# A SwiGLU layer on one core: the two x loads of the head on one queue, the Silu table load ahead of a weight load, and two filler matmuls removed

## The chip, the core and the metric

The kernel runs on one core of a Trainium2 chip. The core has a matrix engine (TensorE, PE in the profile, whose weight loads have a row of their own, PEld), VectorE (DVE), ScalarE (ACT), GpSimd (POOL), SyncE (SP) and 16 DMA engines. A transfer is issued by an instruction on SP, ACT or POOL; each of the three has its own DMA queue (q1, q10 and q0 in the profile), and the same 16 engines serve all three.

The metric is the device time of one execution in microseconds. Before the change it is 163.57 us (median of 3 runs, 163.47 to 163.64).

## The reference

The inputs are bfloat16: `x` is 1 x 2048 x 640, `w_gate` and `w_up` are 640 x 1536, `w_down` is 1536 x 640.

```python
def reference(x, w_gate, w_up, w_down):
    g = _silu(x @ w_gate)
    u = x @ w_up
    return (g * u) @ w_down
```

## The kernel before

The kernel keeps everything on chip: the weights `wg_sb`, `wu_sb`, `wd_sb`, the transposed input `xT` (640 along the partitions, as `KD` = 5 blocks of 128, indexed `kd`), and the transposed product `aT`. The 2048 rows of x are worked in `NSB` = 4 blocks of 512. For each block the loop over `fc` (12 blocks of 128 columns of the weights) makes a gate tile `pg` and an up tile `pu` in PSUM, each by 5 matmuls over `kd` (`proj`, L199). `gate` then has ScalarE take the Silu of `pg` (L216) and VectorE multiply it with `pu` into `aT` (L217). After the 12 blocks the down projection follows (L275 and L304), and the results leave through ScalarE copies and output DMAs. The dot products of the last 4 rows are made on VectorE beside this (L148).

The change lies in the **head**, the first 9 us, in which the first weights and the first rows of x arrive. The first 512 rows of x are taken in two ways. Rows 0 to 255 (two blocks of 128, `PE_X` = 2) are loaded as they are (`load_x`, L86, 160 KB each) and turned by TensorE: five transposes for each block (L190), whose results ScalarE copies to `xT` for `kd` 0 and 1 and VectorE for `kd` 2 to 4 (L195). Rows 256 to 511 come by a DMA that transposes (`turn_x`, L110).

The weights come in column chunks. The first chunk (`fc` 0 and 1) is cut into four transfers at `K_CUT` = 2 (the loop at L120): of the gate weights, `kd` 0 and 1 on SP (128 KB) and `kd` 2 to 4 on ACT (192 KB); of the up weights, `kd` 0 and 1 on POOL (128 KB) and `kd` 2 to 4 on SP (192 KB). The rest follows on SP (L83, L126).

The order on each engine is the order in which the program is written (`keep_order`):

- SP issues: x block 0, the gate part `kd` 0 and 1, the up part `kd` 2 to 4, the transposing load of rows 256 to 511, then the later chunks of the weights, `w_down`, the next x rows and the transposed weights.
- ACT issues x block 1 and the gate part `kd` 2 to 4, then loads the Silu table (by a dummy activation on `ones`, L122), then makes its copies and activations.
- PE runs 20 filler matmuls on `ones` (`warm(N_WARM)`, L177), the ten transposes (L190), 2 more fillers (`warm(N_GAP)`), and the early gate matmuls of L241: `kd` 0 and 1 for `fc` 0 and 1 on 128 columns of x at a time (8 matmuls), and `kd` 2 to 4 on 256 columns (6 matmuls). Then come the up matmuls on the same 256 columns (10, L199), and for each `fc` the gate and up matmuls on the columns 256 to 511 (4 groups of 5, L199). From `fc` = 2 on, the matmuls are 512 columns wide.

What each group needs: a block's transposes need its x load; the 8 matmuls need the gate part `kd` 0 and 1 and ScalarE's copies; the 6 need the gate part `kd` 2 to 4 and VectorE's copies; the up matmuls need both up parts; the columns 256 to 511 need the transposing load.

Of the kernel before, what the change touches and what calls it, by code (L numbers as in the profile page):

```python
# [10 lines left out]
def _body(  # L11
# [8 lines left out]
    nc = tc.nc  # L20
# [3 lines left out]
    ACT = mybir.ActivationFunctionType  # L24
# [12 lines left out]
    SUB = S_BLK // P  # L37
    DA = 512
    Q = 32
    N_WARM, N_GAP = 20, 2  # L40
    T = 4
    WT_STEP = 4
    PE_X = 2
# [35 lines left out]
    def wslice(a, b):  # L79
        return slice(a * P, b * P)  # L80
# [4 lines left out]
    def load_x(eng, c0, c1):  # L85
        eng.dma_start(out=x_sb[:, c0:c1, :], in_=x_v[:, c0:c1, :])  # L86
# [11 lines left out]
    def keep_order(engine):  # L98

        traced = [i for i in nc.cur_bb.bb.instructions if i.engine == engine]  # L100
        for a, b in zip(traced, traced[1:]):
            issue_order(a, b)

    ones = consts.tile([P, 1], bf16)
    silu_first = consts.tile([P, 1], f32)
    nc.vector.memset(ones[:], 1.0)  # L106

    def turn_x(c0, c1):
        s_sl = slice(c0 * P, c1 * P)
        nc.sync.dma_start_transpose(out=xT[:, :, s_sl], in_=xt_v[s_sl])  # L110

    load_x(nc.sync, 0, 1)
    load_x(nc.scalar, 1, 2)
    f_sl = wslice(*W_CHUNKS[0])
    for dst, src, first, second in (
        (wg_sb, wg_v, nc.sync, nc.scalar),
# [2 lines left out]
        for eng, k_sl in ((first, slice(0, K_CUT)), (second, slice(K_CUT, KD))):  # L119
            eng.dma_start(out=dst[:, k_sl, f_sl], in_=src[:, k_sl, f_sl])  # L120
    turn_x(PE_X, SUB)
    nc.scalar.activation(silu_first[:], ones[:, 0:1], ACT.Silu)  # L122
    for a, b in W_CHUNKS[1:]:
        load_w(nc.sync, wg_sb, wg_v, a, b)
        load_w(nc.sync, wu_sb, wu_v, a, b)
# [49 lines left out]
    def warm(n):  # L175
        for _ in range(n):
            nc.tensor.matmul(  # L177
                pw[:, 0:P],
                lhsT=ones[:].broadcast_to([P, P]),
                rhs=ones[:].broadcast_to([P, P]),  # L180
                start=True,
                stop=True,
            )

    def transpose_chunk(c, parts):
        c_sl = slice(c * P, (c + 1) * P)
        for copy, tag, k0, k1 in parts:
            pt = psum.tile([P, k1 - k0, P], bf16, tag=tag, name="pt")
            for kd in range(k0, k1):
                nc.tensor.transpose(  # L190
                    out=pt[:, kd - k0, :],
                    in_=x_sb[:, c, kd * P : (kd + 1) * P],
                    identity=ident[:],
                )
            copy(out=xT[:, k0:k1, c_sl], in_=pt[:])  # L195

    def proj(ps, w_sb, fc, sb, c0, c1):
        for kd in range(KD):
            nc.tensor.matmul(  # L199
                ps[:, c0:c1],  # L200
                lhsT=w_sb[:, kd, fc * P : (fc + 1) * P],
                rhs=xT[:, kd, sb * S_BLK + c0 : sb * S_BLK + c1],
                start=(kd == 0),
                stop=(kd == KD - 1),
            )

    def gu_tiles():
        pg = psum.tile([P, S_BLK], f32, tag="gu", name="pg", bufs=4)
        pu = psum.tile([P, S_BLK], f32, tag="gu", name="pu", bufs=4)
        return pg, pu  # L210

    def gate(pg, pu, sb, fc, n_s):

        s0 = sb * S_BLK
        sg = work.tile([P, S_BLK], f32, name="sg")
        nc.scalar.activation(sg[:, 0:n_s], pg[:, 0:n_s], ACT.Silu)  # L216
        nc.vector.tensor_tensor(  # L217
            out=aT[:, fc, s0 : s0 + n_s], in0=sg[:, 0:n_s], in1=pu[:, 0:n_s], op=ALU.mult
        )

    def head():

        dve, act = nc.vector.tensor_copy, nc.scalar.copy
        split = [(act, "po_a", 0, 2), (dve, "po_b", 2, KD)]
        late = PE_X * P
        (pg0, pu0), (pg1, pu1) = gu_tiles(), gu_tiles()  # L230
        warm(N_WARM)
        transpose_chunk(0, split)
        transpose_chunk(1, split)
        warm(N_GAP)
        early = [(kd, c * P, (c + 1) * P) for c in range(PE_X) for kd in range(K_CUT)]
        early += [(kd, 0, late) for kd in range(K_CUT, KD)]
        for kd, c0, c1 in early:
            for fc, pg in ((0, pg0), (1, pg1)):


                nc.tensor.matmul(  # L241
                    pg[:, c0:c1],
                    lhsT=wg_sb[:, kd, wslice(fc, fc + 1)],
                    rhs=xT[:, kd, c0:c1],
                    start=(kd == 0 and c0 == 0),
                    stop=(kd == KD - 1),
                )
        proj(pu0, wu_sb, 0, 0, 0, late)
        proj(pu1, wu_sb, 1, 0, 0, late)
        for fc, pg, pu in ((0, pg0, pu0), (1, pg1, pu1)):  # L250
            proj(pg, wg_sb, fc, 0, late, S_BLK)
            proj(pu, wu_sb, fc, 0, late, S_BLK)
            gate(pg, pu, 0, fc, S_BLK)
        keep_order(mybir.EngineType.PE)
        keep_order(mybir.EngineType.Activation)
        keep_order(mybir.EngineType.Pool)

    head()
    for sb in range(NSB):
        n_s = S_BLK if sb < NSB - 1 else S_BLK - T  # L260
# [138 lines left out]
def kernel(tc, *args):  # L399
    _body(tc, *args)  # L400
    tc.close()
    tc.compile()
    _trim(tc.nc)
# [30 lines left out]
```

## Time and profile before

| | |
|---|---|
| median of 3 runs | 163.57 us (163.47 to 163.64) |
| the profiled execution's own time | 163.5 us |
| its span, first to last instruction | 162.1 us |
| PE busy | 159.6 us (98% of the span) |
| DVE, ACT, POOL busy | 110.8, 42.8, 1.5 us |
| granted TensorE clock | 1.000 |
| DMA bytes, mean rate | 15.86 MB, 98 GB/s |
| DMA rate from 1.30 to 2.50 us, from 2.50 to 3.50 us | 283, 290 GB/s |

The span starts with SP's first DMA issue and ends with the last instruction; the profiled execution took 1.4 us more than its span. A matmul's duration overlaps that of the next, so what counts on PE is the step from one start to the next. A DMA's time to landing runs from its issue to its last semaphore update.

### The profile page before, as it was taken

How to read it: one execution, taken by the hardware profiler on the slowest of the kernel's cores; microseconds unless marked ns; L12 is line 12 of the kernel's file. 1: busy time of each engine (PE TensorE's matmuls, PEld its weight loads, DVE VectorE, ACT ScalarE, POOL GpSimd, SP SyncE). 2: the span in 40 equal slices, each digit the busy share in tenths (PEclk: the TensorE clock that was granted, in tenths of full speed). 3: DMA queues.
4: the chain of work that ended last, by engine and by line, in shares of the span. 5: the costliest groups of instructions: out<-in, count | busy, mean ns of one | idle time of the engine just before them, and what ended most of it. 6: DMA issues, size and time to landing. Idle time of an engine off the chain costs nothing.

```text
span 162.1 us, 2123 instructions
## 1 busy us (share of the span) xinstructions
PE 159.6 (98%) x800; PEld 78.0 (48%) x800; DVE 110.8 (68%) x249; ACT 42.8 (26%) x74; POOL 1.5 (1%) x7
## 2 busy tenths in 40 slices
PE   9999999999999999999999999999999999999995
PEld 8854444444444444444444444444444444445454
DVE  1052233499569999979919999979964999993000
ACT  5132222112222222221222322221214222222121
POOL 3000000000000000000000000000000000000000
DMA  7999999996179995003110000000320000000212
GB/s 222 250 341 349 361 217 235 199 231 125 34 171 119 250 172 132 4 0 34 65 65 0 4 0 2 0 0 2 62 69 32 0 0 0 0 0 4 50 39 73
DMA packets 42217, 15.86 MB, mean 98 GB/s; under 512 B 33216, under 2 KB 42048, under 8 KB 42208
## 3 DMA queue, kind: packets, MB, share of 16 engines
q1 hardware_dynamic: 33680, 14.75, 38.5%
q10 hardware_dynamic: 8480, 0.85, 3.5%
q8 instruction: 6, 0.10, 0.2%
q0 software_dynamic: 48, 0.13, 0.2%
q14 instruction: 3, 0.02, 0.1%
HBM read 6.88 MB, written 2.62 MB: 59 GB/s over the span
## 4 chain that ended last, share of the span: by engine, by line
PE 96%; DMA 3%; ACTq 0%; DVE 0%; issue 0%
PE pu L199 32%; PE pg L199 31%; PE po_a L304 26%; PE po_t L275 6%; DMA wg_sb<-in_w_gate_dram 3%; PE pg L241 1%; ACTq L86 0%; DVE ot_b L316 0%
## 5 line engine op out<-in xcount | busy, mean ns | idle before, releaser
L199 PE MATMUL pu<-xT,wu_sb 128*128 128x512 bf16 (+2 forms) x250 | 59.7, 370 | 0.0
L199 PE MATMUL pg<-xT,wg_sb 128*128 128x512 bf16 (+2 forms) x240 | 58.5, 374 | 0.0
L217 DVE TENSOR_TENSOR aT<-sg,pu 128x512 bf16<-128x512 f32 (+1 forms) x48 | 32.8, 682 | 32.0 <-PE pu L199 27.5
L216 ACT ACTIVATE sg<-pg 128x512 f32<-128x512 f32 (+1 forms) x48 | 28.6, 596 | 71.0 <-PE pg L199 67.8
L304 PE MATMUL po_a<-wd_sb,aT 128*128 128x512 bf16 (+2 forms) x216 | 42.8, 358 | 0.0
L148 DVE SCALAR_TENSOR_TENSOR prod<-wgT,x_row 128x640 f32<-128x640 bf16 x48 | 39.4, 821 | 1.7 <-DMA wgT<-in_w_gate_dram 0.6
L148 DVE SCALAR_TENSOR_TENSOR prod<-wuT,x_row 128x640 f32<-128x640 bf16 x48 | 39.4, 822 | 1.0
L199 PEld LDWEIGHTS <-wu_sb 128*128 128x128 bf16 x250 | 24.5, 98 | 27.3
L199 PEld LDWEIGHTS <-wg_sb 128*128 128x128 bf16 x240 | 23.5, 98 | 26.9
L304 PEld LDWEIGHTS <-aT 128*128 128x128 bf16 x216 | 20.7, 98 | 21.6
L313 ACT CAST ot<-po_a 128x512 bf16<-128x512 f32 (+1 forms) x17 | 9.5, 560 | 32.0 <-PE po_a L304 20.2
L275 PE MATMUL po_t<-aT,wd_sb 128*128 128x512 bf16 (+1 forms) x48 | 10.4, 366 | 0.0
L275 PEld LDWEIGHTS <-wd_sb 128*128 128x128 bf16 x48 | 4.7, 98 | 5.1
L316 DVE CAST ot_b<-po_a 128x128 bf16<-128x128 f32 x1 | 0.3, 292 | 9.9 <-PE po_a L304 9.9
L284 ACT CAST ot_t<-po_t 128x512 bf16<-128x512 f32 (+1 forms) x4 | 2.2, 558 | 11.6 <-PE po_t L275 11.6
L148 DVE DVE_READ_ACCUMULATOR prod<-wuT,x_row 128x1 f32 x48 | 4.0, 82 | 0.0
L148 DVE DVE_READ_ACCUMULATOR prod<-wgT,x_row 128x1 f32 x48 | 3.9, 82 | 0.0
L286 DVE STREAM_TRANSPOSE ot_q<-ot_t 128x512 bf16<-128x512 bf16 (+1 forms) x4 | 2.7, 677 | 1.7 <-ACT ot_t L284 1.7
L177 PE MATMUL pw<-ones 128*128 128x128 bf16 x22 | 2.7, 313 | 0.3 <-DVE ones L106 0.3
L195 DVE COPY xT<-pt 128x384 bf16<-128x384 bf16 x2 | 0.7, 358 | 3.3 <-PE pt L190 3.3
L177 PEld LDWEIGHTS <-ones 128*128 128x128 bf16 x22 | 2.3, 147 | 0.3 <-DVE ones L106 0.3
L241 PE MATMUL pg<-xT,wg_sb 128*128 128x128 bf16 (+1 forms) x14 | 1.9, 297 | 0.2 <-DMA wg_sb<-in_w_gate_dram 0.2
(16 smaller groups left out, 8.1 us busy)
## 6 DMA issues: line engine op xcount, KB each, us to landing
wd_sb<-in_w_down_dram SPq DMA_DIRECT2D x1, 1920.0 KB, 14.6
out_dram<-ot SPq DMA_DIRECT2D x15, 128.0 KB, 1.7
wg_sb<-in_w_gate_dram SPq DMA_DIRECT2D x2, 640.0 KB, 7.8
wu_sb<-in_w_up_dram SPq DMA_DIRECT2D x2, 640.0 KB, 8.7
x_row<-in_x_dram SPq DMA_DIRECT2D x1, 640.0 KB, 5.0
out_dram<-ot_q ACTq DMA_DIRECT2D x12, 32.0 KB, 2.0
wg_sb<-in_w_gate_dram SPq DMA_DIRECT2D x1, 320.0 KB, 4.4
wu_sb<-in_w_up_dram SPq DMA_DIRECT2D x1, 320.0 KB, 4.9
```

Of the source, the lines that this page charges most:

```text
L148: nc.vector.scalar_tensor_tensor(out=prod[:], in0=wT[:, fc, :], scalar=1.0, in1=x_row[:, t, :], op0=ALU.mult, op1=ALU.mult, accum_out=acc[ ...
L177: nc.tensor.matmul(pw[:, 0:P], lhsT=ones[:].broadcast_to([P, P]), rhs=ones[:].broadcast_to([P, P]), start=True, stop=True,)
L195: copy(out=xT[:, k0:k1, c_sl], in_=pt[:])
L199: nc.tensor.matmul(ps[:, c0:c1], lhsT=w_sb[:, kd, fc * P : (fc + 1) * P], rhs=xT[:, kd, sb * S_BLK + c0 : sb * S_BLK + c1], start=(kd == 0 ...
L216: nc.scalar.activation(sg[:, 0:n_s], pg[:, 0:n_s], ACT.Silu)
L217: nc.vector.tensor_tensor(out=aT[:, fc, s0 : s0 + n_s], in0=sg[:, 0:n_s], in1=pu[:, 0:n_s], op=ALU.mult)
L241: nc.tensor.matmul(pg[:, c0:c1], lhsT=wg_sb[:, kd, wslice(fc, fc + 1)], rhs=xT[:, kd, c0:c1], start=(kd == 0 and c0 == 0), stop=(kd == KD ...
L275: nc.tensor.matmul(po_t[:], lhsT=wd_sb[:, kf, DA:D], rhs=aT[:, kf, sb * S_BLK : sb * S_BLK + n_t], start=(kf == 0), stop=(kf == KF - 1),)
L284: nc.scalar.copy(ot_t[:], po_t[:])
L286: nc.vector.transpose(out=ot_q[:], in_=ot_t[:])
L304: nc.tensor.matmul(po[:], lhsT=aT[:, kf, s0 : s0 + P], rhs=wd_sb[:, kf, c0:c1], start=(kf == 0), stop=(kf == KF - 1),)
L313: nc.scalar.copy(ot[:], po[:])
```

## The change

Three edits in the head. Both x loads are issued by SP, one after the other, so that SP's first gate part, its up part, the transposing load and all that follows there stand one issue later. ScalarE no longer issues an x load: its first instructions are the table load and the dummy activation, and its one early DMA, the gate part `kd` 2 to 4, stands behind them. The two fillers between the transposes and the early gate matmuls are gone. The order on DVE and POOL is the same as before.

```diff
-    N_WARM, N_GAP = 20, 2
+    N_WARM = 20
...
     load_x(nc.sync, 0, 1)
-    load_x(nc.scalar, 1, 2)
+    load_x(nc.sync, 1, 2)
+    nc.scalar.activation(silu_first[:], ones[:, 0:1], ACT.Silu)
     f_sl = wslice(*W_CHUNKS[0])
     for dst, src, first, second in (
         (wg_sb, wg_v, nc.sync, nc.scalar),
...
     turn_x(PE_X, SUB)
-    nc.scalar.activation(silu_first[:], ones[:, 0:1], ACT.Silu)
     for a, b in W_CHUNKS[1:]:
...
         transpose_chunk(0, split)
         transpose_chunk(1, split)
-        warm(N_GAP)
         early = [(kd, c * P, (c + 1) * P) for c in range(PE_X) for kd in range(K_CUT)]
```

## The prediction

> **What bounds the kernel now.** I read the page's busy times and its chain first, then the chain in order of time, then the timeline of the first 7 us, and last the DMA issues of that stretch with their times to landing.
>
> The page: PE, and the chain's shares.
>
> ```profile
> PE   9999999999999999999999999999999999999995
> ...
> PE 96%; DMA 3%; ACTq 0%; DVE 0%; issue 0%
> ```
>
> The chain in order of time (start, length, what):
>
> ```profile
> 0.12 0.41 ACTq L86
> 0.53 0.04 issue
> 0.57 4.49 DMA wg_sb<-in_w_gate_dram
> 5.06 0.05 issue
> 5.11 0.83 PE pg L241 x6
> 5.94 1.09 PE pu L199 x10
> 7.03 0.55 PE pg L199 x5
> ```
>
> PE bounds the kernel, and from 5.11 us on the chain is PE without a hole: an edit in the head changes the end only by moving when that unbroken run starts, or by breaking it. What it hangs on now is ScalarE's gate part (call it G2), issued at 0.57 and landed at 5.06.
>
> The timeline of the head (start, length, engine, line):
>
> ```profile
> 1.04 1.28 ACT L122 ACT_TABLE_LOAD   x1 [1.04 <-issue]
> 1.43 1.95 SPq L110 DMA_TRANSPOSE xT<-in_x_dram  x1
> 2.34 0.20 ACT L122 ACTIVATE silu_first<-ones 128x1 f32<-128x1 bf16 x1
> ...
> 2.59 1.25 PE L190 MATMUL pt<-ident,x_sb 128*128 128x128 bf16 x10
> ...
> 3.62 0.42 PE L177 MATMUL pw<-ones 128*128 128x128 bf16 x2
> ...
> 3.84 1.06 PE L241 MATMUL pg<-xT,wg_sb 128*128 128x128 bf16 x8
> ...
> 5.11 0.83 PE L241 MATMUL pg<-xT,wg_sb 128*128 128x256 bf16 x6 [0.21 <-DMA wg_sb<-in_w_gate_dram]
> ...
> 5.77 1.25 PE L199 MATMUL pu<-xT,wu_sb 128*128 128x256 bf16 x10
> ```
>
> The two fillers take 3.84 - 3.62 = 0.22 us. The 8 early matmuls step by 0.107 us and are through at 3.84 + 0.86 = 4.69; PE then stands 0.42 us until 5.11. The next 6 step by 0.11, twice the columns in the same time.
>
> The DMA issues of the first 3.4 us (last column: us from issue to landing):
>
> ```profile
> wg_sb<-in_w_gate_dram ACTq DMA_DIRECT2D x1, 192.0 KB, 4.5
> wu_sb<-in_w_up_dram SPq DMA_DIRECT2D x1, 192.0 KB, 4.6
> ...
> x_sb<-in_x_dram ACTq DMA_DIRECT2D x1, 160.0 KB, 2.8
> wg_sb<-in_w_gate_dram SPq DMA_DIRECT2D x1, 128.0 KB, 3.1
> wu_sb<-in_w_up_dram POOLq DMA_DIRECT2D x1, 128.0 KB, 4.5
> xT<-in_x_dram SPq DMA_TRANSPOSE x1, 5.3
> ```
>
> Add the issue times of the timeline: x block 1 lands at 0.12 + 2.8 = 2.9, SP's gate part (G1) at 0.46 + 3.1 = 3.56, the up parts at 1.01 + 4.5 = 5.5 (POOL) and 0.92 + 4.6 = 5.5 (SP), the transposed rows at 1.43 + 5.3 = 6.73. Set against what needs them, the up matmuls at 5.77 (their weight load at 5.66) and the gate matmuls on columns 256 to 511 at 6.86, there is little slack behind G2: about 0.1 us at each. This is what I build on.
>
> **The change part by part.**
>
> *SP's queue.* One issue more stands ahead of G1, the up part, the transposing load and all later chunks. Its cost is the step from SP's first issue to its second, 0.46 us. G1 is issued at 0.92, the up part at 1.38, the transposing load at 1.89, the second gate and up chunks at 3.89 and 4.51 instead of 3.43 and 4.05. Those two landed 4.4 and 4.9 us after issue, at 7.8 and 8.95; with 0.46 more, 8.3 and 9.4, against weight loads on PE at 8.94 and 9.91. So the later chunks are covered by 0.5 us or more, if their slip is the whole 0.46.
>
> *Bytes on the DMA engines.* The windows view has them at 283 and 290 GB/s from 1.3 to 3.5 us, share 0.96 and 1.00: they are full, so where a load lands goes by what moves ahead of it. The sum of the head's loads is the same before and after: 2 x 160 + 2 x 128 + 2 x 192 = 960 KB, and 320 KB for the transposed rows. I take SP's and ACT's queue to share evenly while both have work. G1 before: 288 KB of SP's queue (x block 0, G1) and as much of ACT's, 576 KB. After, if ACT issues at once: 448 KB of SP's and all 192 KB of G2, 640 KB. That is 64 KB more, at 290 GB/s 0.23 us: G1 lands at 3.56 + 0.23 = 3.79. Its bounds are 3.3 (G2 starts late and takes nothing) and 3.56 + 0.46 = 4.02. x block 1 had SP's half against it before and has G2 against it now: 2.9, unchanged. G2 before: 352 KB of ACT's and as much of SP's, 704 KB; after, 192 KB and as much of SP's, with x block 0 partly gone ahead: 400 to 560 KB, 0.5 to 1.0 us earlier. One slow engine can hold the last update, so I take half of the middle, 0.4: 4.66.
>
> *ScalarE's DMA behind the table load.* No row of this trace shows a DMA issue behind a running ACT instruction. The lower bound is that it waits for nothing and goes out at about 0.15, where ACT issues its first DMA now. The upper bound is the end of table load and activation, 0.12 + 1.28 + 0.20 and a little = 1.65, which is 1.08 later than 0.57. I take the lower one: the ACTIVATE starts 0.02 us behind the table load's end (2.32, 2.34), less than the 0.03 to 0.04 between ACT's own issues (0.53 to 0.57, 1.01 to 1.04), so it stood ready behind the running load, and what reads ACT's instructions had passed it by then. [...]
>
> *PE.* Without fillers PE is free at 3.62 and waits for G1 at 3.79, so it starts the 8 matmuls at about 3.83 instead of 3.84: the 0.22 us of fillers turn into a wait. The 8 end at 4.69 as before, G2 is there, and the hole of 0.42 closes: the 6 matmuls end between 4.69 + 6 x 0.11 = 5.35 and, should the first still step at half that rate, some 5.6.
>
> *What is late next.* The up matmuls need the up part of POOL, whose issue is unmoved, and SP's. Both land behind the whole 960 KB, 5.5, so their weight load starts at 5.55 to 5.6 instead of 5.66: 0.1 of the 0.42 is left. Ten steps of 0.109 on, at 6.76, the columns 256 to 511 need the transposed rows. They land behind all 1280 KB at 6.73, whose issue has 0.46 us more ahead of it but needs the engines only from about 4 us. With 0.05 us from landing to start, as at G2 (5.06 to 5.11), PE goes on at 6.78 instead of 6.86.
>
> **Sum:** -0.42 (hole) + 0.32 (wait for the up part) + 0.02 (wait for the transposed rows) = -0.08 us against the profiled execution's 163.5 (span 162.1 and 1.4 around it), which is 0.07 under the median of the runs: 163.42, or 163.49 against the median. I say **163.45 us**.
>
> **Rivals.** What a measurement here can tell from no change is about 0.2%, 0.33 us.
>
> 1. *ScalarE's DMA waits for the table load and the activation (slower).* G2 goes out at 1.65. Against a full slip of 1.08 stands that before it also queued behind x block 1. Its landing slips by 0 to 1.08, and the 6 matmuls start where it lands, with nothing to absorb it: 163.5 to 164.6. My middle is 0.4, so 163.9. It decides from a slip of 0.33 on, a landing of G2 after 5.4. Chance 0.28: 0.18 slower, 0.10 within.
> 2. *The transposed rows land later by SP's extra issue (slower).* 6.73 + 0.46 = 7.19, PE starts at 7.24 instead of 6.86: +0.38, 163.88. Against it: full engines, and an issue that runs 1.95 us, from 1.89 to 3.84, before they are due. Chance 0.12: 0.07 slower, 0.05 within.
> 3. *The up parts and the transposed rows come earlier as well (faster).* The last semaphore updates of the head come long after full rate has ended (42 GB/s from 4.90 to 5.10): one or two engines lag. If another order spreads them better, the whole 0.42 is kept: 163.08. Chance 0.20: 0.18 faster.
> 4. *PE's step halves later.* 128 columns step by 0.107 until 4.69, 256 by 0.109 from 5.11, with a granted clock of 1.00 in every window, so the rate doubles in between. If two fillers fewer and a wait of 0.2 delay that, each 256-column matmul costs 0.10 more: 16 of them up to 6.86, at most +1.6, 165.1. Against it: PE is busy from 0.30 on with 20 fillers, which stay. Chance 0.06. [...]
>
> **How the numbers follow.** The forecast has 0.34: 0.31 within 0.2%, 0.02 faster, 0.01 slower. With the rivals: faster 0.20, within 0.48, slower 0.32. The range reaches down to rival 3 (163.08) and up past rivals 1 and 2 (163.9) to about half of rival 1's bound: 163.05 to 164.1. What is left out is rival 4, the worst of rival 1 and a little below rival 3. The forecast alone is 163.3 to 163.65.
>
> **What would show it.** ACT's DMA issue at about 0.2, beside a table load that starts there too, shows the lower bound; one at 1.4 or 1.65 shows rival 1. G2 landed before 4.7 with no hole ahead of the 6 matmuls, a wait for `wu_sb` ahead of the up matmuls, and the gate matmuls on columns 256 to 511 starting at 6.78 show the sum. Those starting at 7.2 on a wait for `xT` show rival 2, at 6.45 rival 3. Steps of 0.21 for 256 columns after 5.1 show rival 4. I am wrong if the landings of the up parts or the transposed rows are not set by the bytes.

## The result, and the profile after

The changed kernel takes **164.38 us** (median of 12 runs, 164.0 to 165.47); the kernel before, run beside it on the same chip, takes 163.52 us (12 runs, 162.97 to 164.04). The ratio is 1.0054 with a 95% interval of 1.0037 to 1.0071: slower by 0.54%, and the medians are 0.86 us apart. The forecast was 163.45 us, no measurable change, with a range up to 164.1. The result lies above that range. (Medians here are over all runs; ratios leave out runs that stand more than 1.5% above the fastest of their kernel, so the two can differ by about 0.1%.)

The profiled execution of the changed kernel took 164.01 us, with a span of 162.6 us, against 163.5 and 162.1 before. It is among the quickest of its kernel, so it shows 0.51 us of the loss.

The page of the changed kernel: PE's slices and the shares of the chain that ended last.

```profile
PE   7899999999999999999999999999999999999995
...
PE 94%; DMA 3%; SPq 1%; DVE 0%; issue 0%
```

PE is still the bound, but its first two slices of some 4 us each have fallen from 9 to 7 and 8: the holes are in the head. The chain in order of time (start, length, what) shows what PE's unbroken run now hangs on:

```profile
1.90 5.45 DMA xT<-in_x_dram
7.35 0.04 issue
7.39 0.71 PE pg L199 x5
```

Before, the chain hung on ScalarE's gate part (landed at 5.06) and ran on PE from 5.11. Now it hangs on the transposed rows, landed at 7.35, and runs on PE from 7.39. Those are the gate matmuls on columns 256 to 511, which stood at 6.86 before: 0.53 us later, the loss of this profile.

The timeline of the changed kernel's head (start, length, engine, line, and in brackets PE's idle time):

```profile
0.12 1.28 ACT L114 ACT_TABLE_LOAD   x1
...
0.25 0.48 ACTq L121 DMA_DIRECT2D wg_sb<-in_w_gate_dram  x1
...
1.90 2.03 SPq L110 DMA_TRANSPOSE xT<-in_x_dram  x1
...
2.42 0.73 PE L190 MATMUL pt<-ident,x_sb 128*128 128x128 bf16 x5
...
3.94 0.45 PE L190 MATMUL pt<-ident,x_sb 128*128 128x128 bf16 x5 [0.79 <-DMA x_sb<-in_x_dram]
...
4.23 1.50 PE L240 MATMUL pg<-xT,wg_sb 128*128 128x128 bf16 x14
...
5.56 0.38 PE L199 MATMUL pu<-xT,wu_sb 128*128 128x256 bf16 x2
...
6.12 1.05 PE L199 MATMUL pu<-xT,wu_sb 128*128 128x256 bf16 x8 [0.17 <-DMA wu_sb<-in_w_up_dram]
...
7.39 0.71 PE L199 MATMUL pg<-xT,wg_sb 128*128 128x256 bf16 x5 [0.22 <-DMA xT<-in_x_dram]
```

Three things are to be seen. ScalarE's DMA goes out at 0.25 beside a table load that runs from 0.12 to 1.40. The transposes of x block 1 wait for their load: a hole of 0.79 us that was not there before. And behind it PE catches up (the up matmuls start at 5.56, before 5.77), only to wait twice more: the eight up matmuls that need SP's up part start at 6.12, and the next group at 7.39. The brackets count to the modelled end of the matmul before; by steps of 0.109 us from start to start the two stretches hold 0.34 and 0.39 us of waiting, and -0.21 + 0.34 + 0.39 = 0.52.

The DMA issues of the changed kernel's first 3.4 us (last column: us from issue to landing, for x block 0 and 1 the middle of the two):

```profile
x_sb<-in_x_dram SPq DMA_DIRECT2D x2, 160.0 KB, 2.9
wg_sb<-in_w_gate_dram ACTq DMA_DIRECT2D x1, 192.0 KB, 3.7
wu_sb<-in_w_up_dram SPq DMA_DIRECT2D x1, 192.0 KB, 4.7
wg_sb<-in_w_gate_dram SPq DMA_DIRECT2D x1, 128.0 KB, 3.2
wu_sb<-in_w_up_dram POOLq DMA_DIRECT2D x1, 128.0 KB, 4.3
xT<-in_x_dram SPq DMA_TRANSPOSE x1, 5.4
```

With the issue times, as in the prediction:

| | forecast | landed | before |
|---|---|---|---|
| x block 1 (issued 0.45; 2 x 2.9 - 2.3) | 2.9 | 3.9 | 2.9 |
| G1 (0.91 + 3.2) | 3.79 | 4.1 | 3.56 |
| G2 (0.25 + 3.7) | 4.66 | 3.9 | 5.06 |
| up part of POOL (1.02 + 4.3) | 5.5 | 5.3 | 5.5 |
| up part of SP (1.38 + 4.7) | 5.5 | 6.1 | 5.5 |
| transposed rows (1.90 + 5.45) | 6.73 | 7.35 | 6.73 |

The windows view, first of before, then of after (busy time of PE, PEld, DVE, ACT and POOL, then the granted clock, the busy share of the DMA engines, and GB/s):

```profile
1.00:2.00 1.00, 1.00 (x13) 1.00 (x11) 0.00 (x0) 0.96 (x1) 0.83 (x1) 1.00 0.90 237
2.00:3.00 1.00, 1.00 (x11) 0.78 (x10) 0.00 (x0) 0.53 (x2) 0.00 (x0) 1.00 0.96 289
3.00:4.00 1.00, 1.00 (x12) 1.00 (x11) 0.49 (x2) 0.74 (x2) 0.00 (x0) 1.00 1.15 351
4.00:5.00 1.00, 0.90 (x9) 0.63 (x6) 0.23 (x1) 0.00 (x0) 0.00 (x0) 1.00 1.60 229
5.00:6.00 1.00, 0.89 (x9) 0.81 (x10) 0.00 (x0) 0.00 (x0) 0.00 (x0) 1.00 0.81 182
6.00:7.00 1.00, 1.00 (x12) 0.90 (x10) 0.00 (x0) 0.00 (x0) 0.00 (x0) 1.00 1.20 307
```

```profile
1.00:2.00 1.00, 1.00 (x13) 1.00 (x11) 0.00 (x0) 0.60 (x2) 0.83 (x1) 1.00 0.82 199
2.00:3.00 1.00, 1.00 (x11) 0.89 (x9) 0.00 (x0) 0.13 (x1) 0.00 (x0) 1.00 0.90 287
3.00:4.00 1.00, 0.21 (x3) 0.07 (x2) 0.36 (x1) 0.25 (x1) 0.00 (x0) 1.00 1.13 286
4.00:5.00 1.00, 0.93 (x14) 0.81 (x15) 0.36 (x1) 0.37 (x1) 0.00 (x0) 1.00 0.95 212
5.00:6.00 1.00, 0.94 (x10) 0.59 (x7) 0.00 (x0) 0.00 (x0) 0.00 (x0) 1.00 1.06 162
6.00:7.00 1.00, 0.88 (x8) 0.80 (x9) 0.00 (x0) 0.00 (x0) 0.00 (x0) 1.00 1.29 292
```

The same bytes are asked for in both kernels, but the engines moved fewer of them: 199 against 237 GB/s in the second microsecond, 286 against 351 in the fourth. From 1 to 7 us that is 1438 KB against 1595, a deficit of 157 KB, and 157 KB at 290 GB/s are 0.54 us. So not only the bytes ahead of a load decide, as I had summed them, but also how early and how well the engines are used.

The DMA view of the stretch from 1 to 3 us in 40 slices of 0.05 us, its rate row, before and then after:

```profile
GB/s 128 205 179 179 230 179 230 230 256 179 230 230 307 282 333 256 231 307 256 318 333 379 359 348 364 318 271 271 266 231 282 261 195 215 276 277 277 277 287 297
```

```profile
GB/s 102 26 179 154 77 0 26 102 154 205 410 410 394 415 359 308 256 225 103 72 113 72 113 113 179 210 215 307 338 353 384 358 374 404 353 374 410 328 348 400
```

After, there is a hole from 1.20 to 1.35 us and a low stretch, 72 to 113 GB/s, from 1.9 to 2.2. The trace's packet records say what stands around them: the first packet of each load. Before: x block 0 at 1.02, x block 1 at 1.50, G1 at 1.99, G2 at 2.32. After: x block 0 at 1.02, G2 at 1.63, x block 1 at 2.15, G1 at 2.80. The loads were issued within 0.6 us before (0.00, 0.12, 0.46, 0.57) and within 0.9 after (0.00, 0.25, 0.45, 0.91), over two queues, yet they start 0.3 to 0.65 us apart, in the order of issue. The packets of neighbours overlap: after, G2's run from 1.63 to 3.22 and those of x block 1 from 2.15 to 3.21.

### The profile page after: what moved, and what is told of

It reads as the page before. It is cut to its first block, busy times and chain, and to the rows that moved or that the text cites. A ratio compares the mean times of both kernels' runs of the same rounds, so it can differ in the third digit from the quotient of the medians.

```text
span 162.6 us, 2119 instructions
## 1 busy us (share of the span) xinstructions
PE 159.1 (98%) x798; PEld 77.1 (47%) x798; DVE 110.8 (68%) x249; ACT 42.8 (26%) x74; POOL 1.5 (1%) x7
## 4 chain that ended last, share of the span: by engine, by line
PE 94%; DMA 3%; SPq 1%; DVE 0%; issue 0%
PE pg L199 31%; PE pu L199 31%; PE po_a L303 26%; PE po_t L274 6%; DMA xT<-in_x_dram 3%; SPq L121 1%; SPq L86 0%; DVE ot_b L315 0%
## 5 line engine op out<-in xcount | busy, mean ns | idle before, releaser
L190 PE MATMUL pt<-ident,x_sb 128*128 128x128 bf16 x10 | 1.2, 267 | 0.8 <-DMA x_sb<-in_x_dram 0.8
```

The lines of the kernel that those rows point to most:

```text
L190: nc.tensor.transpose(out=pt[:, kd - k0, :], in_=x_sb[:, c, kd * P : (kd + 1) * P], identity=ident[:],)
```

## The experiments

The theories that were set against each other:

- **Order of starts (S).** A load's first packet comes some half a microsecond behind that of the load issued ahead of it (0.33 to 0.65 us in the two profiles above), on whichever of SP's and ACT's queues it stands. ACT's gate part, out at 0.25, took the second place, and x block 1 the third.
- **Own queue (Q).** x block 1 is late because it is the second on SP's queue.
- **Fillers (F).** The two fillers kept PE in step, and their absence costs.
- **Table load (T).** ScalarE's early table load disturbs its transfer.
- **GpSimd's part (P).** What makes the second half late is POOL's load: its 4 KB packets took a mean of 0.287 us in the profile of after against 0.180 before, the longest 1.12 against 0.59.
- **PE's rate (C).** Idle time in PE's first microseconds delays the moment from which 256 columns step by 0.109 and not 0.213 us (rival 4 of the prediction).

All kernels compute the whole reference. They are given here with the column that decides: in every profile but one, the time of the execution is the start of the gate matmuls on columns 256 to 511 plus 156.6 to 156.75 us (before 163.5 - 6.86 = 156.64, after 164.01 - 7.39 = 156.62), so what happens in the head is all there is. The exception, experiment 9, has 157.0.

| kernel | x block 1's first packet | GB/s from 3 to 6 us | gate matmuls on 256 to 511 | profiled us | median (runs) | ratio to before, 95% |
|---|---|---|---|---|---|---|
| before | 1.50 | 254 | 6.86 | 163.5 | 163.52 (12) | |
| after | 2.15 | 220 | 7.39 | 164.01 | 164.38 (12) | 1.0054 (1.0037 to 1.0071) |
| 1 before, no fillers | 1.58 | 296 | 6.42 | 163.08 | 163.53 (12) | 1.0012 (0.9987 to 1.0037) |
| 2 before, table load first | 1.50 | 286 | 6.92 | 163.57 | 163.9 (12) | 1.0020 (1.0001 to 1.0039) |
| 3 before, x block 1 on SP | 2.25 | 175 | 7.66 | 164.3 | 164.27 (12) | 1.0073 (1.0039 to 1.0107) |
| 4 after, fillers back | 2.34 | 192 | 7.62 | 164.24 | 164.53 (9) | 1.0064 (1.0036 to 1.0091) |
| 5 after, G2 held | 1.75 | 210 | 10.22 | 166.92 | 166.84 (6) | 1.0184 (1.0143 to 1.0225) |
| 6 after, x in one load | 1.85 | 273 | 6.61 | 163.23 | 163.48 (12) | 1.0012 (0.9997 to 1.0026) |
| 7 after, up part on ACT | 2.20 | 295 | 7.00 | 163.63 | 164.85 (8) | 1.0082 (1.0049 to 1.0115) |
| 8 before, up part on ACT | 1.59 | 264 | 6.82 | 163.42 | 163.41 (12) | 1.0007 (0.9993 to 1.0020) |
| 9 after, fillers between blocks | 2.14 | 193 | 7.70 | 164.72 | 164.69 (7) | 1.0062 (1.0038 to 1.0086) |
| 10 after, x in one load, up part on ACT | 1.87 | 251 | 7.02 | 163.62 | 163.28 (12) | 0.9993 (0.9974 to 1.0013) |
| 11 as 7, with fillers | 1.98 | 283 | 7.04 | 163.71 | 163.86 (12) | 1.0021 (1.0005 to 1.0037) |
| 12 after, G2 behind x block 1 | 1.63 | 270 | 8.48 | 165.1 | 164.66 (12) | 1.0054 (1.0023 to 1.0086) |
| 13 after, POOL's load later | 2.28 | 196 | 7.52 | 164.13 | 164.1 (11) | 1.0062 (1.0036 to 1.0088) |
| 14 as 12, with fillers | 1.72 | 220 | 9.54 | 166.28 | 164.41 (12) | 1.0058 (1.0034 to 1.0083) |

First packets are from the packet records; the rate is that of the DMA view from 3 to 6 us. Where x comes in one load, the first packet of its second half is given.

### 1 to 3: the parts of the change alone

**1. No fillers**, from the kernel before:

```diff
         transpose_chunk(1, split)
-        warm(N_GAP)
```

> The kernel before without the two fillers behind the transposes, nothing else. Theory S (each load's first packet comes some 0.5 us after that of the load issued just ahead of it, on either queue, so it is the order of issue that the change spoiled): the loads are untouched, so 163.5, within 0.2 of before. Rival F (the fillers carried the loss): the whole loss, +0.5 to +0.9, and steps of 0.1 us or more for the first 256-column matmuls. Rival Q (two loads on one queue are slower than on two): as theory S here, 163.5.

Measured 163.53 against 163.51 us. PE's unbroken run even started earlier in the profile, with no loss beside it. The fillers carry nothing of the loss.

**2. Table load first**, from the kernel before:

```diff
+    nc.scalar.activation(silu_first[:], ones[:, 0:1], ACT.Silu)
     load_x(nc.scalar, 1, 2)
...
     turn_x(PE_X, SUB)
-    nc.scalar.activation(silu_first[:], ones[:, 0:1], ACT.Silu)
```

> The kernel before with the Silu table load and the dummy activation ahead of ScalarE's two loads, which stay x block 1 and then the gate part. Theory S: ScalarE's first load goes out about 0.13 us later (0.25 instead of 0.12), still second in the order of issue; x block 1 lands at 2.9 to 3.1, time within 0.2 of before. Rival Q: the same. A rival in which the table load itself takes from the loads (its 1.28 us run beside the first transfers instead of behind their issue): slower by 0.3 or more.

Measured 163.9 against 163.51 us, ratio 1.0020 with bounds of 1.0001 and 1.0039: 0.33 us slower, with 0.02 to 0.64 possible. That is less than the whole loss, but as much as the rival's sign of 0.3. In the profile nothing of the loads is disturbed: x block 1, issued at 0.25 beside the table load, started at 1.50, as before, and landed at 2.65, and the time of that execution is 163.57 us. So the early table load does not delay x block 1; whether it costs something by another way stays open. Three of its twelve runs stand at 165.8 to 165.9.

**3. x block 1 on SP**, from the kernel before:

```diff
-    load_x(nc.scalar, 1, 2)
+    load_x(nc.sync, 1, 2)
```

> The kernel before with x block 1 moved to SyncE's queue behind x block 0, nothing else: ScalarE issues its gate part first, at 0.12, then loads the table; fillers kept. Theory S: the gate part takes the second place, x block 1 the third, its first packet at about 2.1 and its landing at 3.6 to 3.9, the hole between the two blocks' transposes is 0.6 to 0.9 us; the time carries the whole loss, +0.5 to +1.0. Rival Q: the same loss. Rival F: none, within 0.2 of before.

Measured 164.27 us, ratio 1.0073: this edit alone brings a loss as large as all three edits together, with the fillers in place and the table load behind ScalarE's load. x block 1's first packet moved from 1.50 to 2.25, behind G2's at 1.68. The loss shows in another place than in the changed kernel. The chain of this kernel:

```profile
0.91 4.43 DMA wg_sb<-in_w_gate_dram
...
5.38 1.27 PE pg L241 x14
```

G1, now the fourth to start (2.67 instead of 1.99), took 4.43 us to land, and PE waited 1.34 us for it. Most of that is not its late start: each load has 16 updates in the trace's semaphore records, and the last is its landing; of G1's, 14 had come by 4.11, the last two at 5.32 and 5.34. Such gaps of 0.97 to 1.45 us inside one load of SP or ACT also stand in experiments 5, 13 and 14; in the four kernels in which POOL issues no load (7, 8, 10, 11) the longest is 0.49. Which of the later loads pays is thus not fixed.

### 4 to 6: what the loss is not, and how the order can be mended

**4. Fillers back** into the changed kernel:

```diff
         transpose_chunk(1, split)
+        warm(2)
```

> The changed kernel with the two fillers back. Theories S and Q: as the changed kernel, +0.5 to +0.9 against before, since the fillers only fill a wait. Rival F: the loss is gone, within 0.2 of before.

Measured 164.53 us, ratio 1.0064: the loss stays. Theory F falls from both sides.

**5. G2 held** in the changed kernel: the dummy activation writes where G2 will land, so that G2 waits for it and is issued at 1.66, behind SP's x loads, G1 and up part. The two x loads stay on SP.

```diff
-    nc.scalar.activation(silu_first[:], ones[:, 0:1], ACT.Silu)
+    nc.scalar.activation(wg_sb[:, K_CUT, 0:1], ones[:, 0:1], ACT.Silu)
```

> The changed kernel, its dummy activation writing into the place that ScalarE's gate part overwrites, so that this load is issued only when table load and activation are through, at about 1.65 instead of 0.25. Both x loads stay on SyncE's queue. Theory S (starts follow the order of issue on both queues): x block 1 is second again, its first packet at 1.5 to 1.7 and its landing by 3.1, no hole between the two blocks' transposes; the gate part itself lands later, 4.2 to 5.0. Rival Q (second on its own queue is what delays it): x block 1's first packet still at 2.1 or later, landing 3.5 to 3.9, hole of 0.6 to 0.9 us. The time by theory S: 163.5 to 164.0; by Q: 164.2 or more.

The row of the two x loads in this kernel's DMA issues:

```profile
x_sb<-in_x_dram SPq DMA_DIRECT2D x2, 160.0 KB, 2.3
```

2.3 and not 2.9: still second on SP's queue and issued at 0.45 as in the changed kernel, x block 1 started at 1.75 and landed at 2.73, and the ten transposes ran without a hole. So its own queue is not what makes it late; theory Q falls, and the load put ahead of it is what it waits behind. The time, expected at 163.5 to 164.0, is nevertheless the worst of all, 166.84 us, for two reasons that the windows view shows (columns as above):

```profile
6.00:7.00 1.00, 0.13 (x1) 0.11 (x2) 0.00 (x0) 0.00 (x0) 0.00 (x0) 0.97 0.75 164
7.00:8.50 1.50, 1.50 (x8) 1.06 (x7) 0.00 (x0) 0.00 (x0) 0.00 (x0) 0.50 1.20 275
```

G2 landed at 6.8 and PE waited 0.94 and 1.64 us for the gate parts; and then the granted clock fell to 0.50 and the 256-column matmuls stepped by 0.213 us from 6.87 to 10.3, some 16 steps at 0.104 too much.

**6. x in one load**, in the changed kernel:

```diff
-    load_x(nc.sync, 0, 1)
-    load_x(nc.sync, 1, 2)
+    load_x(nc.sync, 0, 2)
```

> The changed kernel with the two x loads as one of 320 KB on SyncE. Theory S: one start fewer ahead of the gate and up parts, each of which starts about 0.5 us earlier than in the changed kernel; all of x lands at 2.6 to 3.0, the transposes start there and run without a hole; 163.2 to 163.7. Rival Q: the same for x, but the loads behind it on the queue as late as in the changed kernel, 163.9 to 164.4.

Measured 163.48 against 163.25 us, ratio 1.0012 with 1 inside the interval: the loss is gone. From the DMA issues and the timeline of this kernel:

```profile
x_sb<-in_x_dram SPq DMA_DIRECT2D x1, 320.0 KB, 3.0
```

```profile
3.01 1.25 PE L189 MATMUL pt<-ident,x_sb 128*128 128x128 bf16 x10 [0.39 <-DMA x_sb<-in_x_dram]
...
5.48 1.25 PE L198 MATMUL pu<-xT,wu_sb 128*128 128x256 bf16 x10
6.61 0.71 PE L198 MATMUL pg<-xT,wg_sb 128*128 128x256 bf16 x5
```

The load of 320 KB lands at 3.0 as a whole, block 0 later than before and block 1 hardly so, and every group behind it finds its data. The fillers are gone here too and the table load comes first; but SP's extra issue has gone with the second load (G1 is issued at 0.51, the transposing load at 1.52). The expectation that the loads behind start half a microsecond earlier was not met: G2, issued at 0.25 as in the changed kernel, had its first packet at 1.96 instead of 1.63, 0.87 us behind that of x, and G1 at 2.75 instead of 2.80. What is mended is that all of x goes ahead of G2.

### 7 to 11: the second half, and PE's holes

**7. The up part on ACT**, in the changed kernel: POOL issues no load any more, ACT issues its part behind G2.

```diff
-        (wu_sb, wu_v, nc.gpsimd, nc.sync),
+        (wu_sb, wu_v, nc.scalar, nc.sync),
```

> The changed kernel with the up part of kd 0 and 1 issued by ScalarE behind its gate part instead of by GpSimd. It asks where the second half of the loss comes from, the late landing of SyncE's up part (6.1) and of the transposed rows (7.35). Theory P (packets of GpSimd's queue hold the engines up; there they took 0.35 to 1.1 us instead of 0.16): no such packets, SyncE's up part by 5.3, the transposed rows by 6.8, 163.7 to 164.0. Rival U (the two up parts hinder each other, whoever issues them): landings as in the changed kernel, 164.2 to 164.6.

The DMA issues of this kernel:

```profile
wu_sb<-in_w_up_dram SPq DMA_DIRECT2D x1, 192.0 KB, 3.9
wu_sb<-in_w_up_dram ACTq DMA_DIRECT2D x1, 128.0 KB, 3.8
...
xT<-in_x_dram SPq DMA_TRANSPOSE x1, 4.5
```

The landings are what theory P had them be: SP's up part 3.9 us from issue instead of 4.7, the transposed rows 4.5 instead of 5.4, with the same issue times and with x block 1 as late as in the changed kernel (first packet 2.20, hole 0.82). The rate from 3 to 6 us is 295 GB/s instead of 220. The profiled execution is level with before, 163.63 us. But the median, expected at 163.7 to 164.0, is not: five of the eight runs stand at 164.7 to 165.7, three at 163.6 to 163.7.

**8. The same in the kernel before**, as the control:

> The kernel before with the up part of kd 0 and 1 issued by ScalarE behind its gate part instead of by GpSimd: the counterpart of the last one. Theory P: the straggling engine of before (the gate part's last update 0.7 us after the others) is gone, the up parts land at 4.6 to 5.0, the transposed rows at 6.2; 163.0 to 163.4. Rival U: as before, 163.5. By theory S this part starts later, as the seventh load, which costs nothing as long as it lands by 5.5.

Measured 163.41 against 163.25 us, ratio 1.0007: no gain there. SP's up part landed at 5.50 and the transposed rows at 6.69, as before. POOL's load costs the kernel before nothing that can be measured.

**9. Fillers between the blocks' transposes**, in the changed kernel, to close the hole of 0.79 us:

```diff
         transpose_chunk(0, split)
+        warm(8)
         transpose_chunk(1, split)
```

> The changed kernel with 8 fillers between the two blocks' transposes, where PE stands 0.8 us for x block 1. The loads are untouched. Of the changed kernel's 12 runs three lie at 165.1 to 165.5, the others at 164.0 to 164.6. Theory C (in the upper ones PE's step halves late or doubles again, because of the hole): the upper cluster thins out, the median falls to 164.0 to 164.3; a profile steps by 0.11 for 256 columns from about 5 us on. Rival (the clusters come from the loads alone): median and spread as in the changed kernel, 164.4. Theory S alone says nothing on it but that x block 1 lands at 3.6 to 3.9 again.

Measured 164.69 us (7 runs, none above 164.83). The hole is closed and the slowest runs are not there, but the median is no better, for the second half is as late as in the changed kernel or later (gate matmuls on 256 to 511 at 7.70).

**10. x in one load and the up part on ACT**, both edits as above, in the changed kernel:

> The changed kernel with x as one load of 320 KB on SyncE and the up part of kd 0 and 1 on ScalarE behind its gate part, so GpSimd issues none. Theory S: x first, the gate parts second and third, landing by 4.0; theory P: up parts at 4.6 to 5.2, transposed rows at 6.2 to 6.4. Together 163.0 to 163.4, at or a little under before. If theory P holds no further than the last pair of runs (there the median did not follow the landings): as x in one load alone, 163.5.

Measured 163.28 against 163.62 us, ratio 0.9993 (0.9974 to 1.0013): level with before, not faster. Over experiment 6 the second edit brings nothing that can be measured.

**11. The up part on ACT and PE kept busy** with 8 fillers between and 4 behind the transposes:

```diff
         transpose_chunk(0, split)
+        warm(8)
         transpose_chunk(1, split)
+        warm(4)
```

> The changed kernel with the up part on ScalarE (no GpSimd load), 8 fillers between the two blocks' transposes and 4 behind them. Without the fillers it had 163.63 in the profiled execution but 164.7 to 165.7 in five of eight runs. Theory C (idle holes on PE cost the step): the upper cluster goes, 163.6 to 163.9. Rival (the clusters come from the loads): as without fillers, 164.8.

Measured 163.86 us, ratio 1.0021. Eight of twelve runs are at or below 163.98, one at 166.38; in experiment 7 five of eight were at 164.7 or above. With the holes filled most of the upper group is gone, as theory C had it.

### 12 to 14: the order mended by itself

**12. G2 behind x block 1**, in the changed kernel: two memsets on VectorE, on the place of G2, delay its issue to 0.94, behind SP's x loads and G1, and leave all other loads.

```diff
     f_sl = wslice(*W_CHUNKS[0])
+    nc.vector.memset(wg_sb[:, K_CUT, f_sl], 0.0)
+    nc.vector.memset(wg_sb[:, K_CUT:KD, f_sl], 0.0)
```

> The changed kernel with two memsets of VectorE on the place of ScalarE's gate part, so that this load is issued behind SyncE's second (after 0.45, at 0.6 to 1.2) instead of ahead of it (0.25). All else as in the changed kernel, both x loads on one queue. Theory S: x block 1 is second, first packet at 1.6 to 1.8, landing by 2.9, the gate part starts 0.5 to 1 us later and lands by 4.5; most of the loss is gone, 163.4 to 163.8. Rival Q: x block 1 late as before, 164.2 to 164.6.

The DMA issues and the timeline of its profiled execution:

```profile
x_sb<-in_x_dram SPq DMA_DIRECT2D x2, 160.0 KB, 2.3
...
wu_sb<-in_w_up_dram SPq DMA_DIRECT2D x1, 192.0 KB, 4.3
...
xT<-in_x_dram SPq DMA_TRANSPOSE x1, 4.9
```

```profile
2.42 1.27 PE L192 MATMUL pt<-ident,x_sb 128*128 128x128 bf16 x10
4.43 2.31 PE L242 MATMUL pg<-xT,wg_sb 128*128 128x128 bf16 x14 [0.73 <-DMA wg_sb<-in_w_gate_dram]
6.53 2.12 PE L201 MATMUL pu<-xT,wu_sb 128*128 128x256 bf16 x10
8.48 0.71 PE L201 MATMUL pg<-xT,wg_sb 128*128 128x256 bf16 x5
```

x block 1 starts at 1.63 and lands at 2.85, and the transposed rows land at 1.90 + 4.9 = 6.8, about as before (1.50, 2.94 and 6.73), although SP issued them as in the changed kernel. For the start of x block 1 that is theory S by its own test. G1, though, lands at 4.4, later than in either kernel (3.56 and 4.1). The time, expected at 163.4 to 163.8, did not follow: the ratio, 1.0054, is that of the changed kernel. Six of the twelve are at 163.39 to 164.21, six at 165.1 to 166.33. The profile is one of the second six and shows why: ten up matmuls take 8.48 - 6.53 = 1.95 us where before they took 1.09. The steps of 256 columns are 0.213 us up to 8.24 and 0.109 from 8.38. Before, this doubling came between 4.6 and 5.1; here PE stood idle for 0.73 us up to 4.43, waiting for G1, and the doubling came only at the end of the up matmuls.

**13. POOL's load later**, in the changed kernel: a memset on the place of POOL's up part moves its issue from 1.02 to 1.71.

```diff
     f_sl = wslice(*W_CHUNKS[0])
+    nc.gpsimd.memset(wu_sb[:, 0:K_CUT, f_sl], 0.0)
```

> The changed kernel with one more instruction on GpSimd, a memset on the place of its up part, so that GpSimd's load is issued about 0.6 us later. If the second half of the loss (up part by SyncE at 6.07, transposed rows at 7.35) comes from GpSimd's load and SyncE's up part starting together, GpSimd's packets stay near 0.16 us, SyncE's up part lands by 5.5, the transposed rows by 6.8, and the time is at or below 164.0 us with x block 1 still at 3.9. If the late landings come from something else (the late start of the second x block itself), the landings stay as in the changed kernel and the time is 164.3 to 164.8 us.

Measured 164.1 against 163.32 us, ratio 1.0062: no better. The chain of its profile:

```profile
1.71 4.49 DMA wu_sb<-in_w_up_dram
...
6.25 1.26 PE pu L200 x10
```

POOL's packets are nearly of their usual length (mean 0.192 us), but the rate from 3 to 6 us is 196 GB/s and both up parts are late. So long packets of POOL are not the cause by themselves, nor is it that the two up parts start together.

**14. As 12, with 8 fillers behind the transposes:**

```diff
         transpose_chunk(1, split)
+        warm(8)
```

> As the kernel in which ScalarE's gate part is issued behind SyncE's second x load (164.66 us, in two clusters of runs), with eight filler matmuls behind the transposes. If the order of starts and TensorE's idle time are the whole of the loss, x block 1 lands near 2.8, the steps of 256 columns are 0.11 us from the up matmuls on, the upper cluster of runs goes, and the median is 163.5 to 163.9 us. If the idle time has no part in it, the median stays near 164.6 us with both clusters.

Measured 164.41 us, where 163.5 to 163.9 was expected; three runs stand at 165.86 or above, two more above 165.2. The fillers did not cover the hole that matters. In the profile, the slowest of the twelve runs, G1 landed only at 5.27, 0.78 us after the last filler had ended, and the steps of 256 columns stayed at 0.213 us up to 9.35. This does not decide theory C, since the hole was only moved.

No kernel here beats the one before; of those that keep the change, experiments 6 and 10 are level with it.

## Why the prediction was wrong

**The step that failed is "bytes on the DMA engines".** It took the engines as full from 1.3 us on and the two queues as sharing them evenly, and put x block 1 at "2.9, unchanged", since G2 now stood against it in place of SP's loads. That was wrong by a whole microsecond: it landed at 3.9. Up to about 2.2 us the loads started one behind the other, in the order of issue over both queues (first packets before at 1.02, 1.50 and 1.99, after at 1.02, 1.63 and 2.15), and the change gave the second place to G2 and the third to x block 1. Experiments 5 and 12 show it: with G2 issued behind x block 1, which stays on SP, x block 1 lands at 2.73 and 2.85. The clue was in the trace of before: 283 GB/s was a mean over 1.3 to 2.5 us, while its 0.05-us slices stood at 128 to 256 until 1.6 us and at 195 to 379 only from there on.

Of the two premises, the even sharing is by an estimate the larger error. Counted in the order of issue, the bytes up to the end of x block 1 go from 320 to 512 KB, which at 290 GB/s is an estimated 0.68 us of its 1.0. Whether a load costs the next a fixed step or one that grows with its bytes, the runs do not separate: the first packets of the x and gate loads followed each other by 0.14 to 0.95 us (all profiles but that of experiment 5, whose G2 is issued late), and by 0.87 and 1.13 us behind the load of 320 KB (experiments 6 and 10).

That this order costs the time as well is less firmly shown. For it stand experiment 3 (one edit, as large a loss) and 6 and 10 (all of x ahead of G2: level with before), though these two also take SP's extra issue away. Experiments 5 and 12 mend x block 1 but not the time, because a gate part then landed later (at 6.8 and 4.4) and PE stepped at half its rate for longer.

In these profiles a queue of its own was no path of its own: the starts came in the order of issue over both queues (1.02, 1.63, 2.15, 2.80 after the change), so that an earlier issue on one queue (G2 at 0.25 instead of 0.57) delayed the load of the other (x block 1, landed at 3.9 instead of 2.9).

**"Late next" failed with it.** The up parts and the transposed rows were to land "behind all the bytes" at 5.5 and 6.73; SP's up part came at 6.1, the rows at 7.35. The prediction named this as what would make it wrong. The deficit of 157 KB by 7 us is 0.54 us of transfer, as much as the loss of the profile. In the profiled execution this half is the whole loss: PE had made good the first hole by 5.56. Every kernel with x block 1 third and POOL's load in place has a low rate from 3 to 6 us (after 220, and 175, 192, 193, 196 in experiments 3, 4, 9 and 13), and without POOL's load it is 295 and 283 (7 and 11). So POOL's load has a part in it. The place of x block 1 alone does not decide: experiments 5 and 14 have 210 and 220 with x block 1 second. What makes the rate low stays open; experiment 13 excludes the simple answers.

**Rival 2 showed its sign without its cause.** Gate matmuls on columns 256 to 511 after 7.2 on a wait for `xT` were its mark, with 163.88 us. But in experiments 7 and 12 SP issued the transposing load at 1.90 as well, and it landed at 6.4 and 6.8. SP's extra issue is not what makes it late.

**ScalarE's DMA behind the table load: right.** It was issued at 0.25 while the table load ran to 1.40 (forecast about 0.15 to 0.2); rival 1, with the highest chance of the slower ones, fell. Here being right did harm: this early issue is what took x block 1's place.

**G2: right in direction, too small.** 0.4 us earlier was forecast, 1.1 came (5.06 to 3.9), for the same reason: G2 was now second. The forecast had halved the gain for a last update that lags. In the semaphore records of before, 15 of G2's 16 updates had come by 4.33 and the last came at 5.06; after, all 16 came from 3.23 to 3.90. That one engine held it is an estimate of the author's.

**PE and its fillers: right that they cost nothing** (experiments 1 and 4), wrong in what PE waits for: the forecast wait was 0.2 us for G1, the measured one 0.79 us for x block 1.

**Rival 4, with a chance of 0.06, may be the other part.** It is not in the profile of the changed kernel, whose 128-column steps are 0.056 us from 3.94 on. But the profiles of experiments 5, 12 and 14 show it: rates that double at about 8.3 and 9.4, or fall back from 6.87 to 10.3. The changed kernel has three of twelve runs above 165, the kernel before two of the 121 that it had beside these kernels; that those three are of this kind was not shown, since no profile caught one. The trace's clock records begin at the doubling or in the hole ahead of it: in eight profiles anywhere from 3.00 (the changed kernel) to 5.57 us after the span's start, and in experiment 12 at 8.28 (six profiles have none); in experiment 5 they read 1.0 from 3.54, 0.5 from 6.95 and 1.0 from 10.36. There the rate fell after holes of 0.94 and 1.64 us with eight matmuls between them; in experiment 12 the steps stayed at 0.213 us up to 8.24 behind a hole of 0.73 us before 4.43. What splits the runs of one kernel into two groups was not shown: no profile here shows one kernel both ways.

**What is accounted for.** The profile's 0.51 us is the late up part and transposed rows. The median's loss is 0.86, and its other 0.35 us is spread among runs that were not profiled; it stays open how much of it is rival 4.

## What to carry to other kernels

In the first microseconds of a kernel list the loads in the order of issue over all queues, count what goes ahead of a load in that order and not queue by queue, and give the first places to what the bound engine needs first. An issue that came earlier on an idle queue was not free here: G2, issued at 0.25 instead of 0.57, took the place of x block 1, which landed at 3.9 instead of 2.9. And one larger load was better than two (ratio to before 1.0012 in experiment 6 against 1.0054 in the changed kernel). After such a change look at the rate of the DMA engines in short slices and at every wait of the head, for the load that pays may be another than the one that was moved (in experiment 3, which moved x block 1, G1 took 4.4 us from issue to landing instead of 3.1).

## What the hardware showed that was not expected

- **Starts in series.** First packets of SP's and ACT's loads came 0.3 to 0.65 us apart though issued 0.1 to 0.5 us apart on two queues, in order of issue: before at 1.02, 1.50, 1.99 and 2.32, after at 1.02, 1.63, 2.15 and 2.80. Behind one load of 320 KB the next came 0.87 us later (experiment 6).
- **GpSimd's packets stretch.** Its 32 packets of 4 KB took a mean of 0.166 to 0.180 us in the five kernels with POOL's load whose rate from 3 to 6 us is 254 GB/s or more (before, experiments 1, 2, 6, 12), and 0.192 to 0.436 us in the seven with 220 or less (after, 3, 4, 5, 9, 13, 14). Which of the two brings the other is not shown. An early first packet (2.70 to 3.32 in six of the seven) goes with it as a tendency: experiments 12 (3.28, 0.174) and 13 (3.85, 0.192) are the exceptions.
- **PE's rate has two levels at a granted clock of 1.00.** 128 columns step by 0.107 or 0.056 us, transposes too, 256 columns by 0.213 or 0.109, and the clock column reads 1.00 for both at the start; only the fall in experiment 5 shows in it, as 0.50. The first clock record of a trace, where there is one, stands between the last slow step and the first fast one (3.00 in the changed kernel, 8.28 in experiment 12).
